# A kernel with block-recurrent attention and a SwiGLU layer: 11 identity products in place of 34, and a new deal of the first stretch and of batch 1

## The chip, the core and the metric

The kernel runs on one core of a Trainium2 chip. The metric is the device time of one execution, in microseconds (us), given as the median of three runs. The core has a matrix engine (TensorE, PE in the profile, with its weight loads as PEld), a vector engine (VectorE, DVE), a scalar engine (ScalarE, ACT), GpSimd (POOL), and the queue of SyncE (SP), which here issues most transfers. Each engine takes its instructions in the order in which the program wrote them.

## The reference

`x` has the shape (8, 8, 512, 64) and `state` (8, 8, 32, 64). For each of 8 batches and 8 heads, the tokens read the state and the state reads the tokens:

```
a     = softmax(x @ state.T / 8);       xread = a  @ state
a2    = softmax(state @ x.T / 8);       sread = a2 @ x
rows of a batch = concat(xread, sread)          # 512 + 32 rows, 8 heads x 64 = 512 columns
xn    = rows / sqrt(mean(rows**2) + 1e-6) * rms_g
out   = (silu(xn @ w_gate) * (xn @ w_val)) @ w_out    # 512 -> 1536 -> 512
```

`w_gate`, `w_val` and `w_out` arrive as 64-bit floats (6 MB each) and are turned into 32-bit floats on the chip.

## The kernel before, in words

**The first stretch (batch 0).** The weights come in 18 pieces of 1 MB: for each of six pairs of hidden tiles one piece of `w_gate`, one of `w_val`, one of `w_out`. At most four raw pieces are in memory; the next load is issued when a piece has been converted. ACT works out the exponents of a piece in three steps (L247, L250, L253), DVE the mantissas and the final value in three (L274, L277, L283). The first piece is dealt with in two halves of 512 columns, all others with 1024. Meanwhile PE, ACT and DVE do the attention of batch 0, in two halves (`first_half`, `second_half`: transposes of x L516, scores L521, softmax L527 to L544, L549, the norm L556 to L575). Then the weights of batch 0 are folded with the state (`own_weights`: eight products L712, which ACT copies into v, L724), each hidden tile takes a gate and a value product (`hidden`: two matmuls L755 each, Silu L761 on ACT, the product with the value L765 on DVE), and each hidden tile is projected at once (`project_as_ready`, four matmuls L962). The attention of batch 1 runs beside this (`tokens_read`: L318, L329, L356, L366 to L467; `states_read`: L605 to L668), and near the end sums of the output weights (`weight_sums` L1005, `weight_quarters` L1117) for the later batches.

**Batches 1 to 7.** Hidden tiles come in pairs by a scheme of seven products instead of eight (`hidden_seven`: products L859, copies L906 to L913 on ACT, sums L922 to L947 on DVE), with sums of v made by POOL (`more_of_v` L739 to L742) and of the attention weights (`slot_sums` L777 to L780). The projection applies such a scheme twice (`project_twice`: products L1163; sums of quarters of the hidden tiles on DVE, L1211 to L1217 and L1222; results L1176, L1203, L1191 to L1196). Seven quarter sums of the output weights are made once, four of them during batch 1 (L1117), stored, and fetched for each outer product. After batch 7 the state rows of all batches are done.

**What sets the order.** The kernel is written as streams: generators of one letter each, whose every step issues a few instructions. Strings of letters say which stream takes its next step; inside them no scheduler reorders anything, so a string is the order of every engine's queue, DMA issues included. `ORDER` is the first stretch, `FIRST` batch 1, `PERIOD` batches 2 to 6, `LAST` batch 7, `STATES` the end. In `ORDER`, `a` and `b` are the halves of batch 0's attention, `A`, `s` and `S` other attention, `e` and `d` the conversion on ACT and DVE, `v` the folded weights, `h`, `t`, `u` products, Silu and gating, `p` and `c` projection and its copies, `k` and `Q` the weight sums, and `w` the start of batch 1. In `FIRST`, `h`, `t`, `u` are products, copies and sums of `hidden_seven`, `p`, `c`, `k`, `o` those of `project_twice`, `a` and `s` the attention of batch 2, `v`, `x` and `w` the folded weights, `q` the remaining quarter sums of the weights, and `f`, `g`, `G`, `l` fetches.

The letter `z` is `keep_awake`: a product of the identity with itself (128x256, L1298; one line earlier after the change) into a PSUM bank that no one reads. The matmuls of one such product show as two records in the profile.

```
def keep_awake():
    ps = fz.tile([P, 2, P], F32, name="f")
    while True:
        TE.matmul(out=ps, lhsT=ident, rhs=ident.unsqueeze(1).to_broadcast([P, 2, P]),
                  start=True, stop=True)
        yield
```

The strings are read in this way:

```
for stream in ORDER:
    ...
    next(streams[stream])
```

Of the kernel before, what the change touches and what calls it, by code (L numbers as in the profile page):

```python
# [22 lines left out]
FLAT = 1793.0  # L23

ORDER = (
    "zzzzzzaaaaazzbbadedabdebezzaadazbbzezeaezbbsabadzzdbsbdzzabazabadszeeazbezdbbzza"
    "bzeadeddAaeevvbAbAdzeaadazaAAebzazszzAsbdaezAzvesddhdsdtehhduddAAdededAzepvvdtdd"
    "dvdhedheeAtuAhepAeedupAdhhddedveAASddepeevptvddhpddeuepdeeeAdtAeheApAsdupAedddvd"
    "pddhAedsAdvtshddAuAedAdvheeStAdeAspSedhhdepsseusthedvppdesAeAdevdvuAdSedAddpAAAd"
    "dSdAeSAAhheApdAtAdASheuvAtvdevdhuhdShhSShtSwtkkuwuskSpkSkkpQpsppwkkkkpQpQQccQwpc"  # L30
    "QQkkQQwwQwwSQQwc"
)

PERIOD = (
# [4 lines left out]
)  # L39

FIRST = (
    "vqahhxtatahqtahahhauhhxuqattuvtqhqquhhthuqhxquuhxhuxhtataquhauxthhthhhququattvtq"
    "aququqahxahfaaatqahxuuxhuGhhhttuahvhtxakhuaxuhusGGgtushauhxuthuhtaaktguufhhftuhu"
    "ushukppuhptppapuucgukklpupkkkpkkppkpkkkakapcppkpkaaapapppcppkfckspkaakksaasppppp"
    "kkpcgpckksppakakakpapkposppakopkpapspskkapoggapkppkpskakaaposwsswwoppxxxxlgxxsfc"
    "ocfoso"
)
LAST = (
    "vhhtfthhthxuhguxhtvvhutuhxfhtuthuhhuhhxtuthfxhtuxtxuhxhuhuvtauhhhthxuuthkxthuhhh"
# [1355 lines left out]
```

## Time and profile before

| | us |
|---|---|
| runs (median; lowest to highest) | 752.05; 749.98 to 752.31 |
| the profiled execution | 748.86 |
| its span, first to last instruction | 746.8 |
| PE busy in the span | 741.1 |
| ACT busy, DVE busy, POOL busy | 379.6, 577.0, 257.7 |
| first stretch, to the first L859 | 133.78 |
| granted TensorE clock, mean | 0.999 |

The profile is of one execution, 3.2 us under the median of the runs; durations below are from it. In it a time is counted from the span's start. A line of the page or of an answer names an instruction by its source line, engine, operation and tiles (output, then inputs), its shape, how often it stands there, and, in brackets, how long the engine stood idle before it and what ended that. Matmul ends are modelled, and matmuls overlap in the pipe, so the time that one costs its queue is the distance between the starts of two neighbours.

### The profile page before, as it was taken

To read this page: it belongs to the slowest core of one execution; us is meant where nothing else is said; L and a number is where in the kernel's file an instruction comes from. 1 tells how busy PE (TensorE), PEld (TensorE's weight loads), DVE (VectorE), ACT (ScalarE), POOL (GpSimd) and SP (SyncE) were. 2 spreads that over 40 slices of the span, in tenths; PEclk is the share of its full clock that TensorE was granted. 3 is DMA by queue.
4 is the path that set the end of the run, shared out by engine and by line. 5 is a ranking of instruction groups with operands and counts; after the bars stand their busy time and mean duration, and the time that the engine had idled before them with its cause. 6 is when DMAs were issued, how large, how long until landed. Compare 5 with 4: busy or idle time off the path is not lost.

```text
span 746.8 us, 14307 instructions
## 1 busy us (share of the span) xinstructions
PE 741.1 (99%) x5624; PEld 598.1 (80%) x5624; DVE 577.0 (77%) x956; ACT 379.6 (51%) x631; POOL 257.7 (35%) x362
## 2 busy tenths in 40 slices
PE   8999999999999999999999999999999999999998
PEld 7734444779977998889878997799878987899996
DVE  4898968799946994699749994699469954798862
ACT  5999971563454724563265526572547336511220
POOL 3100011621293127612473219312851267324500
PEclk9999999999999999999999999999999999999999
DMA  9897934872795188807782488427860883063311
GB/s 293 280 325 246 373 127 173 289 252 79 285 319 167 28 302 255 263 2 277 215 308 48 159 273 294 122 89 283 276 196 1 301 244 129 1 222 117 133 53 28
DMA packets 60994, 146.15 MB, mean 196 GB/s; under 512 B 14848, under 2 KB 31744, under 8 KB 54016
## 3 DMA queue, kind: packets, MB, share of 16 engines
q1 hardware_dynamic: 47808, 125.78, 48.4%
q10 hardware_dynamic: 13120, 19.47, 9.2%
q8 instruction: 44, 0.72, 0.4%
q14 instruction: 22, 0.18, 0.1%
HBM read 116.46 MB, written 28.77 MB: 194 GB/s over the span
## 4 chain that ended last, share of the span: by engine, by line
PE 98%; DMA 1%; SPq 0%; DVE 0%; issue 0%; ACT 0%
PE f L859 40%; PE f L1163 31%; PE pv L755 6%; PE f L962 6%; PE pv L712 3%; PE at L712 3%; PE f L1025 2%; PE f L1298 1%; PE at L648 1%; PE at L454 1%; PE at L356 1%; DMA raw<-in_moe_w_gate_dram 1%; PE at L307 0%; PE pv L521 0%; PE at L329 0%; PE at L622 0%
## 5 line engine op out<-in xcount | busy, mean ns | idle before, releaser
L859 PE MATMUL f<-aT_s,v 128*128 128x256 f32 x504 | 118.5, 381 | 0.0
L859 PEld LDWEIGHTS f<-aT_s,v 128*128 128x128 f32 x504 | 95.2, 191 | 18.1 <-DVE h L1217 4.2
L922 DVE TENSOR_TENSOR g<-g,f 128x512 f32<-128x512 f32 x84 | 56.0, 685 | 63.9 <-PE f L859 52.1
L1191 POOL TENSOR_TENSOR kept<-kept 128x256 f32<-128x256 f32 x28 | 20.8, 744 | 196.1 <-DVE kept L1203 117.4
L859 PE MATMUL f<-aT_t,vs 128*128 128x256 f32 x336 | 86.6, 382 | 0.0
L1176 ACT COPY kept<-f 128x512 f32<-128x512 f32 (+1 forms) x56 | 30.0, 539 | 101.8 <-PE f L1163 101.8
L1163 PE MATMUL f<-w,h 128*128 128x128 f32 x588 | 74.9, 277 | 0.0
L859 PEld LDWEIGHTS f<-aT_t,vs 128*128 128x128 f32 x336 | 63.3, 190 | 11.9 <-issue 3.6
L739 POOL TENSOR_TENSOR vs<-v 128x256 f32<-128x256 f32 x42 | 30.8, 733 | 121.5 <-ACT v L724 121.4
L1163 PEld LDWEIGHTS f<-w,h 128*128 128x128 f32 x588 | 69.9, 192 | 0.4
L913 ACT ACTIVATE hb<-g 128x1024 f32<-128x1024 f32 x42 | 44.5, 1058 | 45.0 <-DVE g L922 44.6
L935 DVE TENSOR_TENSOR hb<-hb,f 128x512 f32<-128x512 f32 (+1 forms) x48 | 31.2, 650 | 26.9 <-PE f L859 26.6
L300 POOL TENSOR_TENSOR ri<-ss,mhalf 128x4 f32<-128x4 f32 (+1 forms) x9 | 9.5, 1052 | 105.4 <-DVE ss L381 72.2
L755 PE MATMUL pv<-aT_s,v 128*128 128x512 f32 x96 | 44.1, 598 | 0.0
L859 PE MATMUL f<-aT_t,v 128*128 128x256 f32 x168 | 43.9, 384 | 0.0
L962 PE MATMUL f<-wo,hb 128*128 128x512 f32 x96 | 43.8, 598 | 0.0
L859 PE MATMUL f<-aT_s,vs 128*128 128x256 f32 x168 | 43.3, 381 | 0.0
L1163 PE MATMUL f<-wo,h 128*128 128x128 f32 x336 | 42.3, 276 | 0.0
L1163 PE MATMUL f<-wo,hb 128*128 128x128 f32 x336 | 42.1, 276 | 0.0
L1163 PEld LDWEIGHTS f<-wo,hb 128*128 128x128 f32 x336 | 40.3, 192 | 0.4
L1163 PEld LDWEIGHTS f<-wo,h 128*128 128x128 f32 x336 | 39.9, 192 | 0.0
L935 DVE TENSOR_TENSOR hb<-hb,c 128x512 f32<-128x512 f32 (+1 forms) x48 | 35.2, 733 | 5.7 <-ACT hb L913 5.5
(230 smaller groups left out, 1648.7 us busy)
## 6 DMA issues: line engine op xcount, KB each, us to landing
w_m<-w_d SPq DMA_DIRECT2D x48, 1024.0 KB
w<-t_d SPq DMA_DIRECT2D x49, 576.0 KB
out_dram<-kept SPq DMA_DIRECT2D x28, 256.0 KB
raw<-in_moe_w_val_dram SPq DMA_DIRECT2D x6, 1024.0 KB
raw<-in_moe_w_out_dram SPq DMA_DIRECT2D x6, 1024.0 KB
w_d<-w_m SPq DMA_DIRECT2D x6, 1024.0 KB
x_b<-in_x_dram SPq DMA_DIRECT2D x6, 1024.0 KB
x_d<-xB ACTq DMA_DIRECT2D x6, 1024.0 KB
```

The source lines that it names most:

```text
L712: TE.matmul(out=pv[e][Ns * j:Ns * j + Ns, :], lhsT=stT_g[b][D * e:D * e + D, j, :], rhs=w[D * e:D * e + D, j].rearrange("p m k f -> p (m k ...
L739: GE.tensor_tensor(out=vs[:, 0], in0=a21, in1=a22, op=ALU.add)
L755: TE.matmul(out=to[0], lhsT=lhs(i, k), rhs=r, start=(i == 0), stop=(i == len(rhs) - 1))
L859: TE.matmul(out=ps[:, i, 0:half], lhsT=l[:, i, :], rhs=r, start=(start and i == 0 and k == 0), stop=(k == len(lhs) - 1), skip_group_check= ...
L913: SE.activation(out=hb[:, 2 * mp:2 * mp + 2, 0:n].rearrange("p m (c t) -> p m c t", c=2), in_=q["g"][:, :, :, 0:half], func=ACTF.Silu if s ...
L922: VE.tensor_tensor(out=to, in0=to, in1=q[ps][:, :, 0:half], op=ALU.add)
L935: VE.tensor_tensor(out=part, in0=part, in1=val, op=ALU.mult)
L962: TE.matmul(out=banks[r], lhsT=hb[:, m, P * r:P * r + P], rhs=wo[:, m, :], start=(m == 0), stop=(m == NM - 1))
L1025: TE.matmul(out=banks[name][:, r, :], lhsT=lhs(k)[:, P * r:P * r + P], rhs=rhs(k), start=(start and r == 0 and k == 0), stop=(k == HM - 1) ...
L1163: TE.matmul(out=to[half][:, slot, :], lhsT=lhs[:, k, :], rhs=rhs[:, k, :], start=(fresh and n in (0, 4) and k == 0), stop=(k == QM - 1), s ...
L1176: SE.copy(of_half(k, i), banks[name][i])
L1191: GE.tensor_tensor(out=k[:, 4:8:3], in0=k[:, 5:6].to_broadcast([P, 2, QD]), in1=k[:, 4:8:3], op=ALU.add)
```

## The change

Two strings are replaced. `ORDER` has 393 letters where it had 416: 11 `z` for 34, and every other letter as often as before, in another order. Its `z` stood at the places 0 to 5, 11, 12, 25, 26 and so on to 151, and now stand at 0, 1, 6, 34, 45, 46, 48, 54, 56, 58 and 66. `FIRST` has the same letters as before, each as often, in another order. `PERIOD`, `LAST`, `STATES` and all functions are as they were.

```
 ORDER = (
-    "zzzzzzaaaaazzbbadedabdebezzaadazbbzezeaezbbsabadzzdbsbdzzabazabadszeeazbezdbbzza"
-    "bzeadeddAaeevvbAbAdzeaadazaAAebzazszzAsbdaezAzvesddhdsdtehhduddAAdededAzepvvdtdd"
-    "dvdhedheeAtuAhepAeedupAdhhddedveAASddepeevptvddhpddeuepdeeeAdtAeheApAsdupAedddvd"
...
+    "zzaaaazabaabbebaaebedbdedadeebbbsazdabaeabsabzzazbdaaezdzbzeebadadzbAeseadAebabA"
+    "AAaddsavesdbbsvsavAabaeAhdthddddeeduedAdAdhApdpdevhedAvvetheetddeAeudhAehtdAAApe"
+    "hAdudeepAddduddpeAAAvAvpAAesAAdpddvedAsdhhtsepueedepddddeAdssheeddpdtddvvhuevhed"
...
 FIRST = (
-    "vqahhxtatahqtahahhauhhxuqattuvtqhqquhhthuqhxquuhxhuxhtataquhauxthhthhhququattvtq"
...
+    "hhthtaaavvqhaaqtahahuquxqtuxqhthqhhthutuhuuqqaahxauahthquqthuthqqxthqhxhGuxqfuhq"
...
```

Three consequences of the new order are used below. On ACT, the first Silu (L761) now stands ahead of the first two steps of the fifth piece's exponents, behind which it stood. On PE, one group L712 of batch 1 and the transpose L318 now stand behind the first L859. In batch 1, DVE's transpose L630 now stands between the second and third step (L1213, L1215) of the fourth quarter sum, where it stood behind the fourth.

More of the change, by code (lines that the diff above doesn't have):

```diff
@@ L25 @@
 ORDER = (
-    "zzzzzzaaaaazzbbadedabdebezzaadazbbzezeaezbbsabadzzdbsbdzzabazabadszeeazbezdbbzza"
-    "bzeadeddAaeevvbAbAdzeaadazaAAebzazszzAsbdaezAzvesddhdsdtehhduddAAdededAzepvvdtdd"
-    "dvdhedheeAtuAhepAeedupAdhhddedveAASddepeevptvddhpddeuepdeeeAdtAeheApAsdupAedddvd"
-    "pddhAedsAdvtshddAuAedAdvheeStAdeAspSedhhdepsseusthedvppdesAeAdevdvuAdSedAddpAAAd"
-    "dSdAeSAAhheApdAtAdASheuvAtvdevdhuhdShhSShtSwtkkuwuskSpkSkkpQpsppwkkkkpQpQQccQwpc"
-    "QQkkQQwwQwwSQQwc"
+    "zzaaaazabaabbebaaebedbdedadeebbbsazdabaeabsabzzazbdaaezdzbzeebadadzbAeseadAebabA"
+    "AAaddsavesdbbsvsavAabaeAhdthddddeeduedAdAdhApdpdevhedAvvetheetddeAeudhAehtdAAApe"
+    "hAdudeepAddduddpeAAAvAvpAAesAAdpddvedAsdhhtsepueedepddddeAdssheeddpdtddvvhuevhed"
+    "ehptedepsdSudhsdhdeddeetseeveSpdAvvASSAudAAAddAedpSepdAdhdAtdAeShdAeddhSdptAdveh"
+    "evveudhAAShhdtuthkkSAukkSupkwkwSkSkwksQkQkpppQQpcQswwpQQQkSQpQcpQccwSwwwQ"
 )
@@ L41 @@
 FIRST = (
-    "vqahhxtatahqtahahhauhhxuqattuvtqhqquhhthuqhxquuhxhuxhtataquhauxthhthhhququattvtq"
[L43 to L46, printed above, removed]
+    "hhthtaaavvqhaaqtahahuquxqtuxqhthqhhthutuhuuqqaahxauahthquqthuthqqxthqhxhGuxqfuhq"
+    "atGuaataasavxhsahhthuthuuhuxthxtavhutkxahkxuqakhauuuthahuhuhuaGxhttkthuuhuhuhtuh"
+    "pugupfhsatupupupukcfppkpppakspppkpkpkkkkcpppkkappppkpsaagapakgakackcoggkspkskcap"
+    "kkkklpppkaaappkpscspakkasapppoappsapfpappkakplasppkakkwswosksgokfpxcpxfppsxwxxcx"
+    "kgoooo"
 )
```

## The prediction

> **What bounds the kernel now.** I read the page first, then the stretches of 20 us, the chain of waits, and the order in time of PE, ACT and DVE in the first 240 us. The page's first part:
>
> ```profile
> PE 741.1 (99%) x5624; PEld 598.1 (80%) x5624; DVE 577.0 (77%) x956; ACT 379.6 (51%) x631; POOL 257.7 (35%) x362
> ```
>
> TensorE has work at every moment, so time can fall only if work leaves its queue and no wait takes its place. By stretches (span, then busy time of PE, PEld, DVE, ACT, POOL, then clock, DMA share, GB/s):
>
> ```profile
> 20.00:40.00 20.00, 20.00 (x110) 14.01 (x109) 17.74 (x26) 19.34 (x25) 1.91 (x2) 1.00 0.89 295
> 40.00:60.00 20.00, 20.00 (x87) 7.54 (x86) 18.87 (x23) 19.51 (x25) 0.00 (x0) 1.00 0.91 323
> 100.00:120.00 20.00, 20.00 (x149) 9.19 (x148) 12.75 (x21) 8.05 (x12) 4.90 (x5) 1.00 0.39 135
> 160.00:180.00 20.00, 20.00 (x127) 17.00 (x126) 19.65 (x37) 12.54 (x21) 5.09 (x8) 1.00 0.23 80
> ```
>
> From 20 to 60 us ACT is as full as PE: it works out the exponents of the weight pieces. From 100 us ACT has time to spare, and in batch 1 (160 to 180) DVE is the full one. The identity products, and how the chain of waits counts them (start, duration, what):
>
> ```profile
> L1298 PE MATMUL f<-ident x68: 378/380/793, 1.8 to 38.7; 128*128 128x256 f32 x68
> 17.05 2.36 PE f L1298 x10
> 30.28 1.73 PE f L1298 x8
> ```
>
> One product is two records: 34 products. Four take 1.73 us in line, 0.43 each, whatever the single record's 0.38 says. All lie before 39 us. The rows that I count from:
>
> ```profile
> 10.02 0.80 ACT L247 ACTIVATE lin<-raw,bounds 128x512 f32<-128x512 int16 x1 [1.40 <-DMA raw<-in_moe_w_gate_dram]
> 32.72 5.45 PE L755 MATMUL pv<-aT_s,v 128*128 128x512 f32 x12
> 35.53 0.60 ACT L761 ACTIVATE t<-pv 128x512 f32<-128x512 f32 x1
> 51.61 3.60 PE L755 MATMUL pv<-aT_s,v 128*128 128x512 f32 x8
> 133.78 1.03 PE L859 MATMUL f<-aT_s,v 128*128 128x256 f32 x4
> 137.68 1.48 DVE L922 TENSOR_TENSOR g<-g,f 128x512 f32<-128x512 f32 x2 [3.95 <-PE f L859]
> ```
>
> ACT's conversions start at 10.02, when the first weights have landed; the first hidden product is at 32.72, its Silu at 35.53; batch 1 begins at 133.78.
>
> **What leaves PE's queue.** 34 - 11 = 23 products of 0.43 us are 9.9 us. Nothing else is added or removed: every other stream has as many steps as before. If no wait came back, the span would be 9.9 us shorter. The new queue also puts one group L712 (1.02) and one transpose L318 (0.11) behind the first L859 instead of ahead of it; that moves 1.15 us (with the gaps) and saves none.
>
> **What comes back as waits.** I walked the new queues of PE, ACT and DVE forward by hand, each instruction at its start-to-start time in the trace (L247 of 1024 columns 1.28, L250 1.10, L253 1.06, copies 0.47, Silu 0.49, 128x512 products 0.858), with 0.36 us from a matmul's slot to a reader and 0.06 from DVE or ACT to PE, as these rows show.
>
> The loads stand ahead of everything else in the same order, so ACT again starts at 10.02. Up to the first Silu ACT had waited 1.15 us in all (0.25, 0.34, 0.56 after that start), so its work was 24.4 us. The new order puts that Silu ahead of L247 and L250 of the fifth piece, 2.38 us: 10.02 + 24.4 - 2.4 = 32.0, and 32.3 with the 0.3 us of waits that remain in my walk. PE then has its first L755 ready at 29.0, held by the v copies (L724) and the normalised aT_s (L575). Up to there PE waits some 6 us, the longest about 2 (16.2 to 18.2, for the softmax on DVE).
>
> From its first to its fourth Silu ACT has 4 L247, 4 L250, 3 L253, 5 copies and 3 Silus: 5.1 + 4.4 + 3.2 + 2.35 + 1.47 = 16.5 us. The fourth starts at 48.9 and ends at 49.5, and the value product of the fourth hidden tile waits for it: 49.6. PE's own queue from 29.0 to there is 19.6 us, so ACT decides by 0.9.
>
> In the old queue the same product is the second pair of the 51.61 row, at 51.61 + 1.72 = 53.3; ahead of it stand, in both queues, the same 14 L755, 6 L962 and two groups L712. **So the first stretch gains 3.7 us of the 9.9**; 6.2 return as waits.
>
> After it I find PE without a gap. The tightest place is L712 of the sixth weight pair: ACT's queue gives its exponents at 98.5, DVE the weights at 99.8, and PE gets there at 101.2. In the tail, POOL's sums vs are done at 126.9 and PE wants them at about 129.9; DVE reaches its first L922 at 128.3 and PE has the sum for it at 135.0 (the moved L712 stands ahead of that sum), so some 6 us cover DVE's 13 us of L1005, L1117 and L339 there; without that cover their excess would fall on PE.
>
> **Two prices not in the trace.** First, the clock. The first records come 0.43 us apart, three in 1.65 us; at 5.34 three take 0.81:
>
> ```profile
> 1.76 1.65 PE L1298 MATMUL f<-ident 128*128 128x256 f32 x3 [1.76 <-POOL ident masks.py:199]
> 5.34 0.81 PE L1298 MATMUL f<-ident 128*128 128x256 f32 x3
> ```
>
> PE runs at half rate until some 2.5 us of work have passed. Six products filled that wait; now two do. If the half rate lasts until the fourth x chunk is transposed, ACT's copy of it moves from 12.1 to 13.4, and with it all behind: 1.3 us. If it ends by 8.3, nothing. I take 0.3. A gain is excluded, as PE can only be slower.
>
> Second, batch 1. From 137.7 to 206 DVE idles 2.5 us in all, and PE finds the quarter sums just made:
>
> ```profile
> 191.77 0.56 DVE L1213 TENSOR_TENSOR h<-h,hs 128x384 f32<-128x384 f32 x1
> 192.38 1.61 PE L1163 MATMUL f<-w,h 128*128 128x128 f32 x12
> ```
>
> The sum ends at 192.3. The new deal puts the 1.24 us transpose L630 between L1213 and L1215 of this very fourth sum, and the matmul L399 some 1 us earlier against DVE's L396. Against that, the first sum is dealt 6 us of DVE work earlier. Bounds 0 and 1.5; I take 0.6. No gain is possible, since PE has no wait there to lose. On SP one weight fetch passes the load of the next x, and the last store of batch 0 passes another fetch; the tightest, of the last pair of batch 1, is issued at about 147 and used at 157, against 152.6 and 163 before: nothing.
>
> **Sum.** -3.7 + 0.3 + 0.6 = -2.8 us. On the profiled execution (748.86 us, of which 746.8 span) that is 746.1; the median of the runs, 752.05, is 3.2 above that execution, so I give 752.05 - 2.8 = 749.2. With the bounds: 748.3 to 751.2. Differences under 0.3%, 2.3 us, can't be told from none here (the three runs spread over 2.3).
>
> **Rivals.** *The clock falls back* (slower). Place: PE from 6 to 29 us, where my walk leaves it a quarter idle in waits of up to 2 us. Price: 1.3 at the start, and the 8.4 us of PE work from 18.2 to 29.0 at half rate are 16.8 in a place for 10.8: up to 6 more. -3.7 + 7.3 + 0.6 = +4.2: 756.2. It decides from about half of that, 3.1 us, at which the gain is gone. For it: half rate is seen where PE starts from rest, and the 23 products had kept the clock at 1.00. Against: a stalled PE at half rate fills its own waits, and 2.5 us of unbroken work brought the full rate back. [...] Chance 0.17, and 0.05 for milder slowdowns of the same sign.
>
> *Batch 1 gives it back* (same). DVE starts its first L922 2.7 us earlier than before and PE its work 3.7, so DVE has 1 us less in hand, and PE meets late sums at several products: 2 to 3.5 us instead of 0.6, so -3.7 + 0.3 + 2.8 = -0.6: 751.4. For: DVE 19.65 of 20. Against: both engines shift together, and DVE's short idles (0.5 twice) can absorb some. 0.18.
>
> *The products were free* (same). Conversion alone sets the end, and the 9.9 us all return: 752.0. For: ACT 19.5 of 20. Against: ACT idles 2.36 us at 105.45 and 8.27 at 126.70 for PE, so PE's backlog ends that stretch. 0.05.
>
> **How the numbers follow.** The forecast with its bounds has 0.55, of which I put 0.45 below -2.3 us and 0.10 above. Faster 0.45; same 0.10 + 0.18 + 0.05 = 0.33; slower 0.22. The range runs from 747.0 (the forecast's lower bound less 1.3 for a median that itself moves by that) to 755.0, short of the clock rival's full price.
>
> **What would show it.** Right: 22 L1298 records; the first L755 near 29 and its Silu near 32.3; PE idle of 5 to 7 us before 50 and almost none after; first L859 near 129; no PE wait over 1 us in batch 1. Wrong: records of L755 or L859 at double spacing after 13 us (the clock); PE waits for DVE's L1213 to L1217 or L396 between 165 and 205; or waits for ACT after 50, which would put my walk of ACT's queue in error.

## The result and the profile after

| | before | after |
|---|---|---|
| median of 22 runs each (us) | 750.94 | 745.68 |
| lowest and highest | 749.42, 754.07 | 744.33, 751.32 |
| profiled execution, its span | 748.86, 746.8 | 747.82, 745.7 |
| first product of batch 1 | 133.78 | 128.33 (1.15 of it by work moved behind it) |

The ratio is 0.9937, with a 95% interval of 0.9923 to 0.995: the change gains about 4.7 us (the medians differ by 5.3), where 2.8 were forecast, and the time is 1.3 us under the low end of the range. The profiled execution of after is 2.1 us above the median of its runs, that of before 2.1 below the median of its own. So the two traces, which differ by 1.1 us, can't be set against each other without asking what each execution met.

The first part of the page of after:

```profile
PE 733.7 (98%) x5578; PEld 590.0 (79%) x5578; DVE 574.5 (77%) x956; ACT 379.0 (51%) x631; POOL 260.5 (35%) x362
```

By stretches (columns as before: span, PE, PEld, DVE, ACT, POOL, granted clock, DMA share, GB/s), and the waits of PE (us in total, times, longest):

```profile
0.00:20.00 20.00, 15.12 (x93) 12.01 (x94) 9.45 (x23) 12.45 (x19) 5.88 (x35) 1.00 0.95 290
20.00:40.00 20.00, 19.06 (x107) 10.81 (x106) 19.66 (x27) 19.87 (x26) 2.70 (x2) 1.00 0.96 311
40.00:60.00 20.00, 20.00 (x77) 8.11 (x76) 17.33 (x26) 19.91 (x25) 0.00 (x0) 1.00 0.84 290
160.00:180.00 20.00, 19.94 (x132) 18.10 (x131) 19.35 (x35) 12.20 (x23) 3.17 (x4) 1.00 0.27 100
200.00:220.00 20.00, 17.57 (x200) 13.80 (x199) 8.01 (x12) 9.77 (x19) 15.87 (x24) 1.00 0.70 264
```

```profile
PE at L647 <- issue: 2.4, 1, 2.4
PE at L479 <- DMA rows<-in_state_dram: 1.8, 1, 1.8
PE f L1297 <- POOL ident masks.py:199: 1.8, 1, 1.8
PE at L548 <- DVE eS L543: 1.3, 1, 1.3
```

PE now has three waits of over a microsecond before 40 us, three more of 0.17 to 0.45 there (5.8 us in all), and one of 2.44 us at the end of batch 1. Elsewhere it has no wait over 0.1 us. The start and the first stretch in order of time (start, duration, what):

```profile
1.76 2.08 PE L1297 MATMUL f<-ident 128*128 128x256 f32 x4 [1.76 <-POOL ident masks.py:199]
8.43 1.58 PE L520 MATMUL pv<-apart,xT 128*128 128x64 f32 x8
10.29 1.00 PE L520 MATMUL pv<-apart,xT 128*128 128x64 f32 x8
9.44 0.77 ACT L246 ACTIVATE lin<-raw,bounds 128x512 f32<-128x512 int16 x1 [0.18 <-DMA raw<-in_moe_w_gate_dram]
28.95 3.67 PE L754 MATMUL pv<-aT_s,v 128*128 128x512 f32 x8 [0.45 <-DVE aT_s L574]
32.05 0.60 ACT L760 ACTIVATE t<-pv 128x512 f32<-128x512 f32 x1
49.14 1.88 PE L754 MATMUL pv<-aT_s,v 128*128 128x512 f32 x4
128.33 1.13 PE L858 MATMUL f<-aT_s,v 128*128 128x256 f32 x4
```

Eight L520 in 1.58 us and then eight in 1.00, and four L515 in 0.86 us from start to start (7.57 to 8.43) and then in 0.45 (9.84 to 10.29): PE works at half rate at first. The first matmuls wholly at full rate start at 9.8 us, against 4.9 in before; such moments are meant below where full rate is said to come. Summed from start to start up to the value product of the fourth hidden tile, the identity products take 7.0 us of PE's queue where they took 17.0, PE idles 5.8 where it idled 2.1, and the transposes, scores and other small products cost 2.1 more, most of it at half rate. -10.0 + 3.7 + 2.1 = -4.2, which is what that value product shows: 49.14, and 53.33 before.

The late wait is a transfer. By the trace's landing marks, the last of four loads of `e` for batch 2 was issued on ACT's queue at 196.20, just behind a fetch of w_m that SP issued at 195.97, and landed at 205.32, 9.1 us later. PE had been ready since 203.1:

```profile
205.51 1.10 PE L647 MATMUL at<-x_b,e 128*32 128x64 f32 x64 [2.44 <-issue]
```

Take these 2.44 us from the execution's 747.82, and it is at 745.4, near the median of 745.68.

### The profile page after: what moved, and what is told of

It is laid out like the page before. It is cut to its first block, busy times and chain, and to the rows that moved or that the text cites. A ratio compares the mean times of both kernels' runs of the same rounds, so it can differ in the third digit from the quotient of the medians.

```text
span 745.7 us, 14219 instructions
## 1 busy us (share of the span) xinstructions
PE 733.7 (98%) x5578; PEld 590.0 (79%) x5578; DVE 574.5 (77%) x956; ACT 379.0 (51%) x631; POOL 260.5 (35%) x362
## 4 chain that ended last, share of the span: by engine, by line
PE 95%; DVE 2%; DMA 2%; issue 1%; ACT 0%; SPq 0%; ACTq 0%
PE f L858 38%; PE f L1162 31%; PE pv L754 6%; PE f L961 6%; PE pv L711 3%; PE at L711 2%; PE f L1024 2%; DMA x_d<-xB 1%; PE at L647 1%; PE at L355 1%; PE at L453 1%; DMA rows<-in_state_dram 1%; PE at L306 0%; PE pv L520 0%; PE at L515 0%
## 5 line engine op out<-in xcount | busy, mean ns | idle before, releaser
L921 DVE TENSOR_TENSOR g<-g,f 128x512 f32<-128x512 f32 x84 | 55.8, 683 | 66.5 <-PE f L858 55.8
L754 PE MATMUL pv<-aT_s,v 128*128 128x512 f32 x96 | 44.3, 599 | 0.4 <-DVE aT_s L574 0.4
```

Source lines behind the costliest of these rows:

```text
L754: TE.matmul(out=to[0], lhsT=lhs(i, k), rhs=r, start=(i == 0), stop=(i == len(rhs) - 1))
L921: VE.tensor_tensor(out=to, in0=to, in1=q[ps][:, :, 0:half], op=ALU.add)
```

## The experiments

Medians here are of 6 to 12 runs; the ratios are to the kernel before, which was run beside each group (750.91 for the first four kernels, 750.45 for the next four, 750.3 for the last four). Each group ran on another chip, so medians of two groups are compared to about 0.6 us. "First product of batch 1" is read in each trace, since nothing behind it moves by the start.

**1. The new ORDER alone.** `FIRST` is that of before.

```
 ORDER = new
-FIRST = "hhthtaaavvqhaaqt..."
+FIRST = "vqahhxtatahqtaha..."
```

> The changed ORDER (11 products, new deal of the first stretch) with the old FIRST. In the two traces the first stretch gains 3.8 us (9.9 us of products leave; 3.7 us come back as waits before 40 us and 2.5 us as matmuls at half rate), and the changed kernel then loses 2.44 us in one wait for a DMA in batch 1. Theory 1, all the gain is in the first stretch and the new FIRST is worth nothing in the median: 3.5 to 4 us faster than before, some 1 us less than the changed kernel shows. Theory 2, the new FIRST also takes away waits that most executions of the kernel before have in batch 1, though its trace does not show them: this kernel keeps those waits, is 3.5 to 4 us faster than before all the same, and the rest of the changed kernel's 4.7 us appears with FIRST alone. Theory 3, two deals that fit only each other: less than 2.5 us faster, with PE waits for DVE in batch 1.

Measured: 745.19 us, ratio 0.9936 [0.9911, 0.9961]. All of the gain is here. The size was missed: the median is 5.7 us below that of before, not 3.5 to 4. Trace against trace, the first product of batch 1 starts 4.44 us earlier than in before (133.78), with the same work ahead of it, and the spans differ by the same 4.4 (742.4 and 746.8):

```profile
129.34 1.03 PE L858 MATMUL f<-aT_s,v 128*128 128x256 f32 x4
```

**2. The new FIRST alone.**

```
 FIRST = new
-ORDER = "zzaaaazabaabbeba..."
+ORDER = "zzzzzzaaaaazzbbadedabdeb..."
```

> The old ORDER (34 products) with the new FIRST. Theory 1: the old queue of PE has no wait from 1.76 us on in its trace and the work is the same, so no gain is possible: 0 to 1.5 us slower. Theory 2 (the new FIRST removes waits that most executions of the kernel before have): 1 to 2 us faster. Theory 3 (FIRST fits only its own ORDER): over 1.5 us slower, with waits for DVE's quarter sums or for the e_d round trip.

Measured: 752.05 us, ratio 1.0015 [0.9999, 1.0031]. Theory 1 holds and theory 2 falls: the new FIRST takes no hidden wait away.

**3. The 23 products taken out, nothing else moved.**

```
 ORDER = that of before, without 23 of its 34 z
```

> The kernel before with 23 of its 34 products taken out and nothing else moved; 11 stay, at about the places where the changed kernel has them. Theory 1, the dealing of the other steps is needed to use the room: ACT's queue up to the first Silu had waited only 1.15 us in the trace of before, so the first Silu comes at most some 1.2 us earlier and the kernel is 0.5 to 2.5 us faster; 7 to 9 of the 9.9 us return as waits before 55 us. Rival, the removal alone does it: 3.5 to 4.5 us faster. Rival, the products were free: within 0.5 us of before.

Measured: 748.62 us, ratio 0.9979 [0.9959, 1.0]: 2.3 us in the medians, 1.2 at the first product of batch 1 (132.62). PE now waits for what the prediction named, ACT's queue in front of the Silu:

```profile
35.17 1.98 PE L754 MATMUL pv<-aT_s,v 128*128 128x512 f32 x4 [0.87 <-ACT t L760]
```

So the room that the products leave is worth less in the old deal; the dealing of the other steps makes more of it usable.

**4. The new deal with 34 products.**

```
 ORDER = the new one, with z at the old places (the last two moved ahead of the first h)
 FIRST = new
```

> The changed kernel (new ORDER and new FIRST) with 34 products instead of 11, at the places in the order where the kernel before has them. Theory 1: PE's total work is that of before, whose queue had no gap, so it can't be faster: 0 to 3 us slower than before, and 4 to 8 us slower than the changed kernel. Theory 2 (new FIRST takes away batch 1 waits of most executions): 1 to 2 us faster than before at best. Rival, the products only fill waits and cost nothing in the new deal: as fast as the changed kernel, 4 to 5 us faster than before.

Measured: 751.51 us, ratio 1.001 [0.9996, 1.0025]. As theory 1 has it, the deal alone gains nothing while PE's queue is full; the products are not free. Removal and deal have to come together.

**5. None of the 11 left.** (On the new ORDER with the old FIRST, as all that follow but the last and number 8.)

```
-ORDER = "zzaaaazabaabbeba..."
+ORDER = "aaaaabaabbeba..."      # no z at all
```

> Changed ORDER without any of its 11 products, old FIRST (so order_only, 745.19 us, less its products). Theory 1, a chain over DVE and ACT sets the first 49 us (in order_only's trace PE waits 5.8 us there and its 11 products take 7.0): removing the rest shifts PE's waits and gains nothing; the half rate now lasts longer into the scores, by up to 2.5 us of PE work, which the x chunks' copies cover for the most part: 0 to 1.5 us slower than order_only. Rival 1, each product still costs its 0.43: 3 to 5 us faster than order_only, near 741. Rival 2, the products hold the clock up through the waits between 5 and 29 us: half rate comes back there, matmuls at double spacing in the trace after 15 us, 3 to 7 us slower than order_only.

Measured: 754.98 us, ratio 1.0076 [1.0046, 1.0106], 9.8 us above order_only. Theory 1 is far off and rival 1 has the wrong sign; rival 2 has the size. The trace, to be set beside the lines of after above:

```profile
7.79 1.81 PE L520 MATMUL pv<-apart,xT 128*128 128x64 f32 x8
12.70 3.52 PE L520 MATMUL pv<-apart,xT 128*128 128x64 f32 x16
33.13 1.96 PE L711 MATMUL f<-w_m,stT_g 64*32 64x512 f32 x16
37.17 4.22 PE L754 MATMUL pv<-aT_s,v 128*128 128x512 f32 x8 [0.19 <-DVE aT_s L574]
```

Sixteen L711 take 1.09 us elsewhere and 1.96 here. In this execution PE does not fall back: from its first matmul at 5.52 to about 38 us it never gets to full rate, not even in the 13 us from 5.5 to 18.8 in which it has no gap and does only transposes and small score products. It gets there with the first wide products, L754. Three of the other five runs have a mean granted clock of 0.989 to 0.995; number 9 shows what such a figure stands for.

**6. Six products ahead of the first transpose.**

```
-ORDER = "zzaaaazabaab..."
+ORDER = "zzzzzzaaaazabaab..."
```

> Changed ORDER with 6 products ahead of the first transpose instead of 2 (15 in all), old FIRST. The first rows land at 5.5 us whatever PE does, so the four added products lie in a wait of 1.7 us. Theory 1, the slow start costs the end nothing because DVE's and ACT's chain starts only at 13 us: within 0.5 us of order_only (745.19), though the score matmuls (2.6 + 4.2 us in order_only against 1.8 + 3.5 in the kernel before) get their old, shorter times back. Rival, the prediction's price of the start (0.3, at most 1.3 us) is real: 0.3 to 1.3 us faster than order_only.

Measured: 744.62 us, ratio 0.9922 [0.9906, 0.9937]; the slowest of its 6 runs took 745.71. Full rate comes at 7.3 us instead of 9.8, and yet the first product of batch 1 is at 129.46, against 129.34 in order_only. The time is near that of theory 1, but its reason is not shown. The six products, at half rate themselves (5.49 us for their twelve records), do not fit into the wait: they hold the first transpose of x to 7.26 us (5.82 in order_only). So PE's scores end no earlier, and DVE's first step of the softmax waits for them; it starts at 12.70 here and at 12.59 in order_only:

```profile
12.70 0.69 DVE L526 TENSOR_REDUCE m<-pv 128x16 f32<-128x512 f32 x1 [0.37 <-PE pv L520]
```

What the half rate alone costs is not separated by this run; number 11 says more. What the median gains over order_only (0.6 us) is not told from noise.

**7 and 8. One letter moved in the later batches**, so that ACT copies g before it waits for the write x_d.

```
 PERIOD = "...vfxutuxhaxhthaghuaxhh..."     # before
 PERIOD = "...vfxutuxhxhtahaghuaxhh..."     # here
```

Number 7, on the new ORDER:

> order_only with one letter moved in PERIOD, the order of the later batches: the first load of xG stands 3 places later, behind ACT's copy of g. In four of the six traces the write x_d took 8 to 10 us to land in one of the batches 2 to 7 instead of 5.3; ACT waits for it ahead of the copy of g, and PE then waits 0.5 to 0.9 us for that copy (batch at 555 us). Theory 1, this run to run wait is a small part of the scatter and common to both kernels: 0 to 1 us faster than order_only, no wait of PE for g in the trace. Rival, ACT's order there is tight: the v copies behind the loads come late instead, and it is 0 to 1.5 us slower.

Number 8, on the kernel before:

> The kernel before with the same letter of PERIOD moved, nothing else. The trace of before had none of these waits of PE and was 2.1 us faster than the median of its runs. Theory 1, most executions of before do have them: 0.5 to 2 us faster than before (749 to 750.4), and the gap between the two kernels, 5.3 us in the medians but 4.4 us in undisturbed traces, falls to about 4.5 between this kernel and period_later. Rival, the extra 2 us of most executions lie elsewhere (the loads at the start): within 0.5 us of before, and the gap to period_later stays above 5.

Measured: 744.34 us, ratio 0.9932 [0.9907, 0.9957], and 750.87 us, ratio 0.9999 [0.9984, 1.0014]. Number 8 lies within 0.5 us of before and the gap between the two stays at 6.5: theory 1 falls for the kernel before, and the 2 us that most of its executions have more than its trace lie elsewhere. Number 7 is not told from order_only (ratio 0.9932 against 0.9936). The two traces show where such time goes. The span of number 8 is 748.5 us, 1.7 more than that of before. In it the twelve records of the first six products take 5.49 us and full rate comes at 7.9 us, not at 4.9, and with the same queue the first product of batch 1 is 0.8 us late:

```profile
1.76 5.49 PE L1298 MATMUL f<-ident 128*128 128x256 f32 x12 [1.76 <-POOL ident masks.py:199]
134.57 1.03 PE L859 MATMUL f<-aT_s,v 128*128 128x256 f32 x4
```

The other 0.9 us lie in batch 1, where PE waits 0.71 us at 144.6 for a copy of g (L906).

Number 7's profiled execution took 750.06 us, though its other five took 744.1 to 745.0. It has no longer wait than order_only, and this:

```profile
13.32 3.51 PE L520 MATMUL pv<-apart,xT 128*128 128x64 f32 x16
24.11 2.02 PE L1297 MATMUL f<-ident 128*128 128x256 f32 x6
25.97 1.03 PE L555 MATMUL pv<-aT_s,gram 128*128 128x256 f32 x4
34.69 3.67 PE L754 MATMUL pv<-aT_s,v 128*128 128x512 f32 x8 [0.45 <-DVE aT_s L574]
```

Half rate until 25.3 us instead of 9.8; L754 at 34.69 instead of 28.93; the first product of batch 1 at 135.09, 5.75 us later than in order_only. Nothing in the program differs up to there. Of the kernels with the new ORDER as it is, 6 of 37 executions lie above 750 (after 3 of 22, order_only 2 of 9, this one 1 of 6); this trace is the only one of them that was seen from inside. The mean granted clock of all six is 1.0, so none of them shows a loss of full rate like that of number 9, whose traced execution has 0.995. Number 3, which also starts with two products, has two of 12 executions 4 and 6 us above its median.

**9 and 10. Which of the 11 count.**

```
 ORDER = the new one with only its first 3 z      # number 9
 ORDER = the new one without its first 3 z        # number 10
```

> Changed ORDER with only the three products ahead of 7 us (the eight between 14 and 22 us left out), old FIRST. Theory A, what the products do is to bring PE to full rate early: in order_only full rate came at 9.8 us, in no_products only at 38 us and 9.8 us later at the end. If the first three are what counts, full rate comes near 10 us and holds: within 0.7 us of order_only (745.19). Theory B, the later products keep PE from falling back in the waits between 14 and 29 us: matmuls at double spacing again after 15 us, 3 to 9 us slower than order_only. Theory C, each product costs its 0.43 us: 3 us faster than order_only.

> Changed ORDER with only the eight products between 14 and 22 us (the three ahead of 7 us left out), old FIRST. Theory A: half rate lasts through the scores as in no_products until the block of products at 16 to 26 us, as in the one slow execution caught in period_later's trace (full rate at 25.3 us, everything behind 5.75 us later): 4 to 7 us slower than order_only, near 750. Theory B (the later ones count): within 1 us of order_only.

Measured: 749.69 us, ratio 0.9994 [0.9964, 1.0024], runs from 745.3 to 755.6; and 749.16 us, ratio 0.998 [0.9965, 0.9995]. Both medians lose 4 to 4.5 us against order_only, though 5 of the 12 runs of number 9 take 745.3 to 747.0. In the traces the first product of batch 1 comes at 130.90 and 133.12, 1.6 and 3.8 us later than in order_only; this much is the products'. The spans are 2.6 and 1.0 us longer beyond that, with waits in later batches for copies of g and a fetch of w_m (1.7 and 0.7 us), which may be scatter. So both parts are needed, each for its own reason. Without the later eight, full rate comes at 10.0 us and is lost again in a wait of 3.44 us:

```profile
14.62 0.49 PE L491 MATMUL f<-stT 64*128 64x128 f32 x4
18.55 1.09 PE L548 MATMUL at<-ident,eS 128*128 128x128 f32 x4 [3.44 <-DVE eS L543]
20.32 2.07 PE L555 MATMUL pv<-aT_s,gram 128*128 128x256 f32 x4 [0.68 <-ACT aT_s L551]
24.09 1.03 PE L555 MATMUL pv<-aT_s,gram 128*128 128x256 f32 x4
```

Here the granted clock (third figure from the end) falls as well. It was 1.00 up to 16 us and 0.50 between the two rows below; so the share of 0.87 in the first puts the fall at 16.7 us, and that of 0.71 in the second the return near 23.6:

```profile
16.00:17.00 1.00, 0.00 (x0) 0.00 (x0) 1.00 (x3) 1.00 (x3) 0.00 (x0) 0.87 1.05 410
23.00:24.00 1.00, 0.32 (x3) 0.08 (x2) 1.00 (x2) 0.72 (x2) 0.00 (x0) 0.71 0.87 275
```

Without the first three, half rate lasts until the block of later products, as theory A has it:

```profile
16.24 1.96 PE L584 MATMUL at<-xT,stT 64*32 64x512 f32 x16
18.12 1.22 PE L1297 MATMUL f<-ident 128*128 128x256 f32 x2
22.17 0.60 PE L548 MATMUL at<-ident,eS 128*128 128x128 f32 x4
```

**11. Waits filled.**

```
-ORDER = "zzaaaaz..."  and "...zzaz..." ahead of the wait at 17 us
+ORDER = "zzzzzzaaaaz..."  and three z more ahead of that wait
```

> Changed ORDER with 6 products ahead of the first transpose instead of 2, and 3 more in PE's wait at 17.0 to 18.4 us (18 in all), old FIRST. They lie in waits of 1.8 and 1.3 us. [...] Rival, products beyond the waits cost 0.43 each: 0.4 to 1.5 us slower than six_at_start.

Measured: 744.9 us, ratio 0.9924 [0.9907, 0.9941], highest 745.57. As six_at_start: the products at the waits cost nothing, and the three more bring nothing, that the median shows. The trace prices the start, though. Full rate happened to come at 6.5 us, 0.8 earlier than in number 6, DVE's first step of the softmax starts 0.5 earlier than there, and so does the first product of batch 1 (128.97 against 129.46):

```profile
12.21 0.69 DVE L526 TENSOR_REDUCE m<-pv 128x16 f32<-128x512 f32 x1 [0.37 <-PE pv L520]
```

In this trace, in that of number 6 and in that of order_only PE's first L548, which waits for this softmax, starts at 18.00, 18.50 and 18.38, and batch 1 begins 110.96 or 110.97 us later in all three. So a later start of the scores is not hidden in waits: it reaches batch 1 in full. Here a wait of 1.19 us for a copy of g in batch 2 then takes the gain back.

**12. The changed kernel with six at the start.**

```
-ORDER = "zzaaaazabaab..."
+ORDER = "zzzzzzaaaazabaab..."
 FIRST = new
```

> The changed kernel whole (new ORDER, new FIRST) with 6 products ahead of the first transpose instead of 2. Set against six_at_start (744.62, same ORDER, old FIRST) it prices the new FIRST alone. Theory 1, the new FIRST costs what its trace shows in batch 1: 0.5 to 1 us slower than six_at_start, more in executions where the last load of e lands late (2.44 us in the changed kernel's trace). Rival, the new FIRST is worth something with its own ORDER: 0.5 to 1.5 us faster than six_at_start.

Measured: 744.52 us, ratio 0.9921 [0.9903, 0.9939], against 744.62 for six_at_start: with its own ORDER the new FIRST neither costs nor gains anything that 6 runs each can show. Its trace has no wait of PE over 0.1 us behind 50 us. From the first product of batch 1 to that of batch 2 it takes 81.71 us, 1.15 of them the work that was moved there; that leaves 80.56, and order_only takes 80.57. The last load of e was issued at 194.81, ahead of the fetch of w_m (195.80) and not behind it; it landed after 4.8 us, at 199.59, 3.2 us before its use.

Its median is among the lowest of all, 1.2 us under that of the change as it stands. This kernel and numbers 6 and 11 have no execution above 746.4 among 18. Whether the executions above 750, 1 in 6 with the new ORDER as it is, are gone for good, 18 are too few to say.

## Why the prediction was right and wrong

**Right: what bounds it, and that the gain is a part of 9.9 us.** Twenty-two L1297 records, 10.0 us out of PE's queue (9.9 forecast); the first L754 at 28.95 (29.0), the first Silu at 32.05 (32.3), PE idle of 5.8 us before 50 (5 to 7), the first product of batch 1 at 128.33 (near 129), and no wait for ACT after 50. *The products were free* fell with number 4.

**Wrong: the terms of the sum.** Trace against trace, order_only gains 4.44 us; the sum said 2.8.

- "-3.7" for the first stretch was -4.44, with the half rate's price in it. The step that failed is "the value product of the fourth hidden tile waits for it: 49.6 ... so ACT decides by 0.9". ACT's fourth Silu started at 48.36 instead of 48.9: the first Silu was already 0.25 us early, and from there ACT's queue took 16.3 us where the walk had 16.6. PE's own queue from the first L754 to that product took 20.2 us and not 19.6 (28.95 to 49.14, without a wait). So PE's own queue sets this product, at 49.14 and not at 49.6. This is 0.5 of the 0.74; the rest lies behind it, where the same matmuls up to batch 1 take 80.2 us in order_only and 80.45 in before, with no wait in either. That ACT started at 9.44 in after and not at 10.02 is not the reason: it waited 0.80 us for PE's transposes right behind, and in numbers 12 and 11 it started at 10.03 and reached the first Silu at 31.89 and 31.68, earlier still.
- "I take 0.3" for the clock at the start: half rate lasted to 9.8 us, beyond the 8.3 that was the free bound, and yet ACT's copy of the fourth x chunk came at 11.77 (order_only 11.75), ahead of the 12.1 of the walk. So against the walk this term was 0, because the walk had that copy too late. Free the slow start is not: number 11, with full rate at 6.5 us, begins batch 1 0.4 us ahead of order_only.
- "I take 0.6" for batch 1 was 0: numbers 12 and 6 differ by 0.1 us, and batch 1 takes 80.56 and 80.57 us in the traces of number 12 and order_only. The wait of 2.44 us in the trace of after is none of the waits that were weighed (the L630 transpose, L399, SP's fetches), but the landing of a load on ACT's queue behind a fetch on SP's. I had looked at what each queue is moved past and not at what is in flight from the other one. It is no constant price: number 12, in the same order, did not wait.

0.74 + 0.3 + 0.6 = 1.64 is the whole difference between 4.44 and 2.8.

**Wrong: the base.** "752.05 is 3.2 above that execution, so I give 752.05 - 2.8" took the excess of the median over the profiled execution to be the same in both kernels. It was 1.1 too high for a start, since the 22 runs have their median at 750.94. And the rest is not common to both. In before PE's queue has no gap over 0.34 us behind 1.76 us, so each us more at half rate delays everything by up to half a us; full rate came at 4.9, 5.8, 7.2 and 7.9 us in the four traces with the old start, and the profiled one was the earliest. That this explains the 2.1 us between the trace of before and the median is not shown: the most that the start is seen to cost is 0.8 us (number 8), and another 0.9 in that trace lies in batch 1. Of the 3.5 us between 749.2 and the measured 745.68, the terms are 1.6, the median of three runs 1.1, and the excess that the changed kernel does not share 0.8; where this last part lies stays open. On the scale of the profiled execution, the forecast of 746.1 was within 0.4 us of the measured median, but by luck: the gain was forecast 1.6 us too small, and that median lies 1.2 us above the undisturbed execution of order_only (744.52).

What sets the moment of full rate is not shown: with one and the same queue up to it, it came at those four moments with the old start, and at 9.8 and 25.3 us with the new one (order_only and number 7). The stretch at half rate in number 9 lasted some 6.9 us (16.7 to 23.6).

**The rival of the clock: place and size right, mechanism half right.** It had 0.17, and 6 of 37 executions with the new ORDER are above 750. Its price was 7.3 us; the one that was seen lost 5.75. It is not a fall back in the waits, as the rival said, but a full rate that comes 15 us late. The step "2.5 us of unbroken work brought the full rate back" failed: with the old start the half rate lasted 3.1 us in the trace that the prediction was read from and up to 6.1 in the others, and in no_products 13 us of unbroken work, transposes and small score products, did not end it. If the other five executions above 750 are like the one that was seen, it strikes one in six and moves the median little; at 750 to 751 us they take as long as before and not longer.

At full rate, waits of 1.3 us (order_only) and 2.44 us (after, at 203 us) cost no clock: four L548 right behind the first take 0.63 us, sixteen L711 just behind the second 1.09. The one of 3.44 us did (number 9: four L548 in 1.09 us), though the clock fell at 16.7 us, when PE had been idle for 1.6 us only (since 15.11). So these runs show no length of a wait from which on it falls. Nor do they show which work ends the half rate: in number 5 it held over transposes (four L515 in 1.06 us, against 0.60 at full rate), and over L520 and L584, which are none (sixteen L584 in 1.96 us, against 1.09).

**Batch 1 gives it back**, 0.18, did not happen: DVE's L921 started at 134.48, 3.2 us earlier than before, and no wait for the quarter sums appeared.

## What to carry to other kernels

Filler products did two things at once here: they occupied a queue, 0.43 us each at full rate, and they brought the matrix engine to full rate and held it there (it came at 9.8 us with the 11 and at about 38 with none; without the later eight the granted clock fell to 0.50 for a time). The price of removing them was not linear: from 34 to 11, with a new deal, gained 5 us, from 11 to none lost 10. Keep those that lie in a wait which is there anyway (here at the very start, and ahead of the wait that was 3.44 us long without them), and take out those with real work behind them, together with a new order of the engine that becomes late next. Then ask whose queue sets the next product, and count that queue as carefully as the one that was late before. And before a sum is carried from a profiled execution to a median, ask what that execution was spared, and whether the changed kernel would pay the same.

## What the runs showed of the hardware

- The granted clock of the profile's rows showed the loss of full rate in number 9, but not the half rate at the start. It reads 1.00 from 0 to 40 us of no_products, where sixteen L711 take 1.96 us against 1.09; in number 9, where full rate was had and lost, it reads 0.87 and 0.71 in the two rows above and 0.50 between them. Half rate at the start was seen in the records' own durations alone.
- One program, the same queue: full rate at 9.8 us in the traces of after and order_only and at 25.3 in number 7, with 5.75 us between them at the first product of batch 1.
- Transfers of one kind took very different times: in the trace of after, three loads of e landed 4.5 to 4.9 us after issue, and the fourth 9.1, issued 0.2 us behind a fetch of 1 MB of w_m; in number 12, issued 1.0 us ahead of that fetch, the fourth took 4.8. The write x_d of number 4 took 5.1 us for one batch and 10.1 for another; why is not shown.
